# A new table of the order of all steps, and a new set of GpSimd's steps, in a fused attention, mixer and FNet kernel

## The chip, the cores and the metric

The kernel runs on one core of one Trainium2 chip. The metric is the device time of one execution in microseconds (us). A core has five engines that matter here, each with its own instruction queue, worked off strictly in order: TensorE (PE in the profile, with its weight loads as PEld), VectorE (DVE), ScalarE (ACT), GpSimd (POOL), and SyncE (SP), which here only issues DMAs. Engines wait for each other and for DMAs through semaphores. SBUF is the on-chip memory that holds operands, PSUM the one that TensorE writes its sums to.

## What is computed

Three stages, one after the other, in float32. The scale of q and k in the inputs is raised, which changes no shape.

```python
def _attn_ref(q, k, v, cap):                 # (4, 12, 448, 64)
    scores = np.matmul(q, k.transpose(0, 1, 3, 2)) / np.sqrt(64)
    scores = cap * np.tanh(scores / cap)     # cap 30
    attn = np.exp(scores - np.max(scores, axis=-1, keepdims=True))
    attn = attn / (np.sum(attn, axis=-1, keepdims=True) + 1e-09)
    return np.matmul(attn, v)

def _moe_ref(x, w_tok1, w_tok2, w_ch1, w_ch2):   # x (4, 448, 768)
    h = np.maximum(x.transpose(0, 2, 1) @ w_tok1, 0.0) @ w_tok2
    u = x + h.transpose(0, 2, 1)
    return u + np.maximum(u @ w_ch1, 0.0) @ w_ch2      # 768 -> 1536 -> 768

def _moe2_ref(x, w_ch1, w_ch2):
    u = x + np.real(np.fft.fft(np.fft.fft(x, axis=1), axis=2))
    un = (u - mean(u)) / np.sqrt(var(u) + 1e-06)       # over the 768
    return u + np.maximum(un @ w_ch1, 0.0) @ w_ch2     # 768 -> 3072 -> 768
```

## The kernel before

The kernel doesn't issue its instructions where the stages are written. The stages first record steps in a list; a step is one instruction or a few of one kind (one DMA, one vector operation, three or six matmuls), with the tiles that it reads and writes. There are 4196 steps, numbered in the order of recording. `Plan.run` then goes through the table `ORDER` and emits step after step; where a step may run on VectorE or on GpSimd, it goes to GpSimd if its number stands in the set `POOLED` and to VectorE otherwise. Since every engine works off its queue in order, `ORDER` alone sets what stands ahead of what on each engine, and an instruction that waits holds up all that stands behind it on its engine. Tile buffers are handed out in that order too.

```python
for k in ORDER:
    o = self.ops[k]
    ...
    o.fn("P" if k in POOLED else next(e for e in o.engines if e != "P" or len(o.engines) == 1))
```

The names that the rest needs:

- *Matrix products.* Each float32 operand is split into a high and a low part, and each product is three matmuls of 448 columns (`mm3`, lines 403 to 405): high weight by high data, high by low, low by high. `wh` and `wl` (or two tiles `raw`, `p`) are the weight parts, `u`, `r` and `y` data tiles, `mm` a PSUM tile of two halves of 448.
- *Weights.* A step on SP loads them (`raw<-in_m_dram`, line 464). Three ScalarE steps (line 431, `cv`, `raw`) and one VectorE step (line 472) rebuild their values; another pair of steps splits them into the two parts. Parts that are needed again are written to DRAM and fetched back (`kept`, lines 513 and 517).
- *Attention.* Scores `sc` (line 629), tanh on ScalarE (`t<-sc`, line 617), the maximum over partitions on GpSimd (`mb<-m`, line 669), the subtraction on VectorE, exp on ScalarE (line 677), then the product with v (`av`, line 727).
- *Output sums.* Twelve tiles `z` of 128 x 2 x 448 (z_76 to z_87 in the lists) hold the running result. What a second product of a layer leaves in PSUM is added to them by VectorE (`z<-mm,z`, here called a gather; a helper at line 434 records this and every other tensor_tensor, on VectorE and GpSimd alike). A PSUM tile is free for the next product when it has been gathered. At the end `z<-z` steps add pairs of tiles, and `store` (line 1335) writes each tile out, the last of them in two halves.
- *FNet.* `u<-mm,r` at line 1722 and `r<-y,r` at line 1735 are VectorE steps that form data tiles from transform sums; the normalisation stands between them and the last layer.

Of the kernel before, what the change touches and what calls it, by code (L numbers as in the profile page):

```python
# [58 lines left out]
class Op:  # L59
# [6 lines left out]
    2, 0, 3, 54, 4, 68, 69, 5, 1, 6, 55, 56, 7, 8, 10, 9, 57, 11, 12, 14, 13, 15, 20, 21, 58, 22, 16, 18, 23, 17, 19,  # L66
    73, 71, 30, 31, 59, 72, 74, 75, 77, 76, 78, 26, 81, 79, 32, 60, 29, 24, 27, 85, 25, 80, 28, 82, 33, 36, 34, 37,
    86, 39, 87, 95, 35, 38, 40, 121, 122, 70, 61, 88, 124, 41, 83, 42, 43, 84, 62, 44, 63, 45, 64, 46, 126, 96, 97,
    65, 47, 125, 66, 127, 48, 50, 130, 128, 91, 98, 89, 92, 49, 67, 94, 51, 138, 99, 93, 131, 129, 90, 52, 134, 132,
    106, 101, 139, 102, 140, 53, 104, 133, 135, 100, 103, 105, 141, 144, 197, 123, 196, 269, 172, 199, 136, 107, 108,  # L70
    137, 110, 109, 173, 174, 175, 207, 111, 142, 148, 145, 176, 149, 150, 151, 146, 177, 112, 200, 143, 115, 113, 178,
    114, 116, 147, 205, 117, 159, 154, 186, 188, 206, 208, 118, 120, 187, 189, 119, 152, 155, 203, 201, 204, 202, 153,
    190, 193, 272, 209, 270, 198, 179, 213, 214, 215, 157, 180, 191, 181, 156, 182, 210, 158, 216, 192, 223, 183, 217,
    160, 161, 211, 184, 194, 163, 212, 162, 218, 219, 164, 274, 165, 273, 275, 195, 224, 225, 185, 220, 322, 323, 271,
    787, 168, 166, 167, 169, 221, 226, 278, 170, 276, 234, 229, 171, 227, 279, 247, 249, 277, 248, 250, 230, 232, 286,
    222, 282, 280, 251, 254, 788, 789, 790, 281, 283, 228, 231, 284, 325, 235, 255, 285, 233, 256, 296, 287, 288, 297,
    298, 236, 327, 289, 292, 299, 302, 238, 252, 237, 239, 261, 253, 290, 791, 293, 240, 291, 792, 262, 326, 328, 241,
    267, 243, 333, 329, 265, 242, 295, 793, 244, 300, 339, 303, 334, 268, 294, 301, 330, 257, 245, 331, 340, 246, 305,
    304, 332, 306, 258, 341, 342, 794, 384, 324, 783, 510, 786, 383, 307, 308, 309, 337, 335, 795, 310, 338, 311, 336,
    345, 343, 346, 349, 350, 312, 386, 388, 344, 313, 387, 389, 266, 314, 316, 390, 392, 263, 259, 351, 315, 348, 317,  # L80
    352, 457, 385, 456, 347, 373, 375, 393, 391, 355, 318, 394, 396, 353, 374, 358, 319, 356, 320, 321, 376, 400, 401,
    402, 354, 260, 395, 397, 359, 357, 796, 360, 461, 398, 361, 399, 797, 362, 459, 403, 410, 411, 412, 404, 363, 405,
    364, 406, 413, 416, 365, 366, 460, 462, 264, 409, 407, 380, 367, 369, 465, 463, 368, 414, 370, 473, 466, 408, 464,
    415, 371, 377, 467, 471, 372, 474, 417, 419, 475, 509, 458, 378, 381, 468, 418, 434, 420, 472, 421, 422, 469, 423,
    518, 476, 425, 436, 470, 426, 512, 479, 379, 798, 382, 435, 477, 437, 482, 483, 484, 480, 485, 513, 519, 424, 427,
    448, 514, 516, 446, 430, 428, 643, 511, 570, 571, 486, 515, 517, 449, 478, 481, 447, 526, 527, 429, 528, 431, 487,
    489, 529, 438, 432, 520, 488, 521, 439, 490, 433, 492, 440, 524, 494, 522, 491, 523, 493, 525, 495, 496, 532, 535,
    530, 536, 537, 538, 533, 498, 497, 575, 573, 499, 503, 441, 539, 542, 500, 574, 576, 534, 531, 442, 501, 444, 577,
    579, 502, 540, 504, 545, 443, 587, 578, 445, 541, 580, 547, 581, 583, 505, 588, 543, 589, 506, 508, 507, 582, 544,
    546, 560, 562, 584, 450, 548, 549, 585, 590, 550, 451, 586, 551, 593, 645, 696, 572, 644, 646, 552, 648, 452, 558,  # L90
    591, 561, 594, 563, 596, 597, 598, 599, 595, 647, 649, 553, 592, 654, 650, 554, 660, 555, 600, 453, 655, 651, 603,
    564, 652, 454, 556, 653, 559, 601, 604, 661, 662, 557, 606, 656, 658, 602, 605, 565, 657, 659, 455, 607, 663, 670,
    566, 664, 671, 672, 609, 608, 610, 698, 697, 611, 665, 612, 699, 701, 613, 666, 673, 676, 700, 614, 702, 567, 617,
    615, 703, 707, 669, 667, 674, 616, 618, 679, 677, 668, 704, 708, 621, 623, 681, 705, 709, 619, 678, 710, 675, 706,
    680, 622, 624, 713, 620, 714, 715, 625, 682, 683, 711, 716, 626, 568, 684, 685, 712, 627, 569, 723, 724, 725, 717,
# [190 lines left out]
    3010, 3014, 3017, 3063, 3073, 3076, 3110, 3128, 3134, 3174, 3177, 3193, 3209, 3215, 3236, 3239, 3273, 3276, 3378,  # L286
    3385, 3409, 3434, 3446, 3456, 3501, 3517, 3519, 3521, 3524, 3539, 3552, 3564, 3574, 3577, 3589, 3655, 3661, 3664,
    3665, 3696, 3743, 3774, 3802, 3808, 3812, 3815, 3827, 3852, 3865, 3877, 3899, 3908, 3918, 3933, 3945, 3946, 3949,
    3951, 3952, 3981, 4018, 4065, 4115, 4121, 4142, 4166, 4181,
}  # L290


# [1857 lines left out]
```

## Time and profile before

| | us |
|---|---|
| median of 3 runs | 1377.07 |
| range of the runs | 1375.84 to 1378.19 |
| the profiled execution | 1376.16 |
| its span | 1374.4 |
| TensorE busy in the span | 1325.2 |
| VectorE, ScalarE, GpSimd busy | 1044.3, 763.7, 434.3 |
| mean granted TensorE clock, as a share of full | 0.989 |

The profiled execution took 1.8 us more than its span, which goes from the first to the last instruction that the profile shows. The last matmul ends at 1362.2 us in the span.

In rows of a timeline, the first two numbers are the start and the duration in us, then come engine, line, operation, output<-inputs and shape; in square brackets stand the idle time of the engine just before and what ended it. Matmuls overlap, so a busy TensorE is a queue of matmuls that begin one every 0.2 us.

### The profile page before, as it was taken

The numbers are of one execution on the slowest core, as the hardware profiler recorded it, in microseconds if no ns is written. First come the engines' busy times: TensorE is split into PE (matmuls) and PEld (weight loads), VectorE is DVE, ScalarE is ACT, GpSimd is POOL, SyncE is SP. The second block draws the span as 40 slices with busy tenths as digits, with TensorE's granted clock in tenths as the row PEclk, the third lists the DMA queues.
The fourth block names the chain that finished last, engine by engine and source line by source line (L and its number), as shares of the span: only waits on it lengthen the run. The fifth ranks groups of instructions, "written<-read, shape, count | busy, mean of one in ns | idle before, by whom it ended". The sixth has DMA issues, their size and how long they took to land.

```text
span 1374.4 us, 18462 instructions
## 1 busy us (share of the span) xinstructions
PE 1325.2 (96%) x7230; PEld 1098.7 (80%) x7230; DVE 1044.3 (76%) x1078; ACT 763.7 (56%) x926; POOL 434.3 (32%) x217
## 2 busy tenths in 40 slices
PE   7999999999999999999999999998989999999995
PEld 2345454599989899999889999998978889999984
DVE  6998988756656655878998895675899646865996
ACT  6888777687676566455444344543453453543431
POOL 3524344222120222101122544225551225324421
PEclk8999999999999999999999999999999999999998
DMA  4313211047798788887767623546463733333322
GB/s 147 95 64 142 68 41 55 1 164 252 278 315 295 261 313 308 294 300 255 252 235 249 246 98 117 177 164 205 139 227 134 260 117 93 126 103 112 107 69 81
DMA packets 74041, 239.18 MB, mean 174 GB/s; under 512 B 8322, under 2 KB 9730, under 8 KB 73826
## 3 DMA queue, kind: packets, MB, share of 16 engines
q1 hardware_dynamic: 73952, 238.00, 50.9%
q8 instruction: 57, 0.93, 0.3%
q14 instruction: 30, 0.25, 0.1%
q10 hardware_dynamic: 2, 0.00, 0.0%
HBM read 171.74 MB, written 69.56 MB: 176 GB/s over the span
## 4 chain that ended last, share of the span: by engine, by line
PE 67%; DVE 18%; ACT 7%; DMA 4%; issue 3%; SPq 0%; POOL 0%; DVEq 0%; ACTq 0%
PE mm L403 18%; PE mm L404 18%; PE mm L405 18%; DVE z L434 5%; PE av L727 3%; DVE m L434 3%; DMA raw<-in_m_dram 2%; PE sc L629 2%; DVE r L434 2%; ACT cv L431 2%; DVE u L434 2%; DVE t L434 1%; PE av L758 1%; PE mx L870 1%; ACT t L677 1%
## 5 line engine op out<-in xcount | busy, mean ns | idle before, releaser
L434 DVE TENSOR_TENSOR z<-mm,z 128x896 f32<-128x896 f32 (+1 forms) x205 | 198.4, 984 | 90.6 <-PE mm L405 85.0
L404 PE MATMUL mm<-u,wh 128*128 128x448 f32 x630 | 230.7, 366 | 0.5 <-DVE u L1722 0.5
L403 PE MATMUL mm<-u,wh 128*128 128x448 f32 x570 | 208.9, 366 | 0.9 <-issue 0.5
L405 PE MATMUL mm<-u,wl 128*128 128x448 f32 x570 | 208.3, 365 | 0.0
L403 PE MATMUL mm<-r,wh 128*128 128x448 f32 x504 | 185.6, 368 | 8.8 <-DVE z L434 8.8
L405 PE MATMUL mm<-r,wl 128*128 128x448 f32 x504 | 185.0, 367 | 0.0
L434 POOL TENSOR_TENSOR p<-p 128x768 f32<-128x768 f32 (+1 forms) x42 | 86.1, 2052 | 266.5 <-DMA kept<-p 98.7
L404 PE MATMUL mm<-r,wh 128*128 128x448 f32 x450 | 165.5, 368 | 1.3 <-DVE r L946 0.9
L669 POOL PARTITION_ALL_REDUCE mb<-m x48 | 105.3, 2244 | 156.2 <-DVE m L434 156.2
L404 PEld LDWEIGHTS mm<-u,wh 128*128 128x128 f32 x630 | 118.6, 188 | 10.3 <-DVE u L1722 0.7
L431 ACT ACTIVATE r<-mm 128x896 fp32r<-128x896 f32 (+5 forms) x86 | 70.4, 829 | 100.8 <-PE mm L405 68.9
L403 PEld LDWEIGHTS mm<-u,wh 128*128 128x128 f32 x570 | 107.3, 188 | 10.6 <-issue 0.8
L405 PEld LDWEIGHTS mm<-u,wl 128*128 128x128 f32 x570 | 107.2, 188 | 8.9
L403 PEld LDWEIGHTS mm<-r,wh 128*128 128x128 f32 x504 | 94.9, 188 | 19.5 <-DVE z L434 9.0
L431 ACT ACTIVATE cv<-raw 128x768 bf16<-128x768 int8 (+2 forms) x76 | 67.8, 892 | 73.9 <-DMA raw<-in_m_dram 48.9
L434 POOL TENSOR_TENSOR wl<-wl,wh 128x768 fp32r<-128x768 f32 x26 | 51.5, 1984 | 161.7 <-ACT wh L431 131.2
L405 PEld LDWEIGHTS mm<-r,wl 128*128 128x128 f32 x504 | 95.1, 189 | 8.1 <-POOL wl L434 0.3
L404 PEld LDWEIGHTS mm<-r,wh 128*128 128x128 f32 x450 | 84.8, 188 | 10.0 <-DVE r L946 2.4
L472 DVE SCALAR_TENSOR_TENSOR p<-raw 128x768 int32<-128x768 int32 x48 | 49.6, 1033 | 53.8 <-ACT raw L431 51.9
L434 DVE TENSOR_TENSOR t<-t,mb 128x1344 f32<-128x1344 f32 x48 | 79.1, 1662 | 4.5 <-POOL mb L669 4.4
L629 PE MATMUL sc<-qr 64*128 64x448 f32 x288 | 70.4, 594 | 9.7 <-ACT t L617 8.9
L431 ACT ACTIVATE raw<-raw 128x768 fp32r<-128x768 f32 x52 | 43.3, 839 | 64.4 <-DMA raw<-kept 64.4
(243 smaller groups left out, 3074.2 us busy)
## 6 DMA issues: line engine op xcount, KB each, us to landing
kept<-p SPq DMA_DIRECT2D x96, 384.0 KB, 4.8
raw<-in_m_dram SPq DMA_DIRECT2D x48, 767.6 KB, 5.5
wl<-kept SPq DMA_DIRECT2D x88, 384.0 KB, 3.8
raw<-kept SPq DMA_DIRECT2D x52, 384.0 KB, 3.1
raw<-in_c_dram SPq DMA_DIRECT2D x24, 767.6 KB, 5.9
p<-kept SPq DMA_DIRECT2D x30, 384.0 KB, 4.0
qr<-in_qk_dram SPq DMA_DIRECT2D x23, 448.0 KB, 4.1
wh<-kept SPq DMA_DIRECT2D x24, 384.0 KB, 4.4
```

The source lines that it names most:

```text
L403: T.matmul(out=dst, lhsT=wh, rhs=xh, start=first, stop=False, skip_group_check=more)
L404: T.matmul(out=dst, lhsT=wh, rhs=xl, start=False, stop=False, skip_group_check=more)
L405: T.matmul(out=dst, lhsT=wl, rhs=xh, start=False, stop=last, skip_group_check=more)
L431: pl.op(a(n), lambda e: A.activation(out=out(), in_=src(), func=func, **kw), reads, writes)
L434: pl.op(engs, lambda e: eng[e].tensor_tensor(out=out(), in0=in0(), in1=in1(), op=op), reads, writes)
L472: pl.op(v(cols), lambda e: V.scalar_tensor_tensor(out=value(I32), in0=raw()[:rows, :cols, 0], scalar=5, in1=field(), op0=ALU.logical_shift ...
L629: T.matmul(out=ps()[:, k, :S], lhsT=qr()[d, S + c * 128:S + (c + 1) * 128], rhs=qr()[d, :S], start=True, stop=True)
L669: pl.op({"P": 1.9}, lambda e, k=k: P.partition_all_reduce(mb()[:, k], mx()[:, k], 128, bass_isa.ReduceOp.max), [mx, mb], [kb], hold=0.75)
L677: pl.op(a(KC * S, 0.1), lambda e, k=k: A.activation(out=tl()[:, :, k], in_=tl()[:, :, k], func=AF.Exp, scale=cap_sb[:, 0:1]), [tl, "cap"], ...
L727: T.matmul(out=ps()[d, :S], lhsT=vv()[:, KC * p + c, d], rhs=tl()[:, c, hd], start=(c == 0), stop=False, skip_group_check=True)
L758: T.matmul(out=ps()[32 * k:32 * k + 32, :S], lhsT=ones[:, 0:32].bitcast(F32) if c < KC else half_ones[:, p], rhs=tl()[:, c, hd] if c < KC ...
L870: T.matmul(out=ps()[:, :S], lhsT=channels_of(rt()[:, tb, c], kc % NJ), rhs=wt[:, tb, :], start=False, stop=last, skip_group_check=True)
```

## The change

Two tables are replaced, `ORDER` and `POOLED`; no other line differs. TensorE and ScalarE carry out the same steps in another order, and SP issues the same DMAs in another order. GpSimd has 212 steps where it had 211, VectorE 1035 where it had 1036: some steps go to GpSimd that did not, and about as many come back.

```diff
 ORDER = [
-    2, 0, 3, 54, 4, 68, 69, 5, 1, 6, 55, 56, 7, 8, 10, 9, 57, 11, 12, 14, 13, 15, 20, 21, 58, 22, 16, 18, 23, 17, 19,
...
-    4165, 4160, 4115, 4166, 4150, 4184, 4161, 4149, 4155, 4190, 4167, 4168, 4186, 4171, 4187, 4191, 4192, 4151, 4157,
-    4169, 4139, 4170, 4163, 4172, 4156, 4188, 4162, 4193, 4194, 4185, 4173, 4174, 4175, 4189, 4195,
+    2, 0, 3, 54, 4, 68, 69, 1, 6, 8, 7, 9, 55, 10, 11, 56, 12, 14, 13, 15, 57, 20, 21, 22, 58, 16, 18, 23, 17, 19, 71,
...
+    4148, 4114, 4165, 4115, 4166, 4162, 4150, 4149, 4161, 4184, 4155, 4190, 4191, 4186, 4167, 4168, 4171, 4187, 4192,
+    4193, 4151, 4157, 4169, 4139, 4170, 4163, 4172, 4156, 4188, 4194, 4185, 4195, 4173, 4174, 4175, 4189,
...
 POOLED = {
...
-    729, 806, 808, 814, 824, 866, 893, 930, 955, 967, 984, 1029, 1115, 1134, 1145, 1152, 1191, 1204, 1334, 1354, 1377,
+    729, 806, 808, 822, 845, 866, 893, 930, 955, 984, 999, 1017, 1074, 1115, 1134, 1145, 1152, 1191, 1202, 1204, 1334,
```

The order shows in three places.

**ScalarE at the start.** Its first steps, before and then after. `t<-sc` and `te<-sc` are tanh of scores, `cv<-raw`, `cv<-cv`, `raw<-cv` and `w1h<-raw` belong to the first mixer weights, which a DMA brings, and `t<-t,cap_sb` is exp.

```order
L431 ACTIVATE cv_307<-raw_291 112x512 [waits DMAHW3_49]
L431 ACTIVATE cv_307<-cv_307 112x512 [waits Activation_49]
L617 ACTIVATE t_310<-sc_304,scl_75 128x896 [waits DVE_49,PE_49]
L617 ACTIVATE t_310<-sc_312,scl_75 128x896 [waits PE_49]
L431 ACTIVATE raw_291<-cv_307 112x512 [waits Activation_49]
```

```order
L617 ACTIVATE t_308<-sc_302,scl_75 128x896 [waits DVE_49,PE_49]
L617 ACTIVATE t_308<-sc_305,scl_75 128x896 [waits PE_49]
L431 ACTIVATE cv_311<-raw_291 112x512 [waits DMAHW3_49]
L617 ACTIVATE t_308<-sc_313,scl_75 128x896 [waits PE_49]
L431 ACTIVATE cv_311<-cv_311 112x512 [waits Activation_49]
```

The two steps on the mixer weights, which stood ahead of the first tanh, now stand behind the second and the third. Some fifteen steps further on, one tanh (`t_387<-sc_376` before, `t_382<-sc_370` after) stood behind the first exp and now stands ahead of it.

**VectorE in the FNet stage**, before and then after. `r_8054<-r_8054,r_8004` before and `u_8056<-u_8056,r_7982` after are the same step, a difference of two tiles fetched from DRAM; z_79 is gathered right behind it in both.

```order
L434 TENSOR_TENSOR z_81<-mm_8032,z_81 128x448 [waits PE_49]
L434 TENSOR_TENSOR r_8054<-r_8054,r_8004 128x896 [waits DMAHW7_49,DMAHW2_49]
L434 TENSOR_TENSOR z_79<-mm_8042,z_79 128x448 [waits PE_49]
L434 TENSOR_TENSOR wl_8050<-wl_8050,wh_8049 128x768 [waits DMAHW5_49,Activation_49,Pool_49]
L434 TENSOR_TENSOR z_80<-mm_8042,z_80 128x448 [waits PE_49]
```

```order
L434 TENSOR_TENSOR r_8068<-mm_7997,u_7840 128x896
L434 TENSOR_TENSOR wl_8054<-wl_8054,wh_8053 128x768 [waits DMAHW0_49,Activation_49]
L434 TENSOR_TENSOR u_8056<-u_8056,r_7982 128x896 [waits DMAHW3_49,DMAHW1_49]
L434 TENSOR_TENSOR z_79<-mm_8085,z_79 128x448 [waits PE_49]
L434 TENSOR_TENSOR r_7982<-u_8056 128x448 [waits DVE_49,Pool_49]
L434 TENSOR_TENSOR raw_7980<-raw_7980 128x768 [waits DMAHW2_49,Activation_49]
L434 TENSOR_TENSOR raw_8051<-raw_8051 128x768 [waits DMAHW7_49,Activation_49]
L434 TENSOR_TENSOR u_8158<-mm_8073,y_8061 128x896 [waits PE_49]
```

Before, the product that fills the other half of mm_8042 (three matmuls by three, TensorE's next step) needs the gather of z_79 done. After, TensorE's product behind this gather waits for an earlier one, and 15 steps of three matmuls of the first layer stand behind it until the first that needs `u_8158`, the last row shown.

**VectorE at the end**, its last rows before (but the very last) and then after. mm_11183 before and mm_11187 after are the PSUM tile whose two halves end in z_84, the tile that is stored in two halves.

```order
L434 TENSOR_TENSOR z_80<-mm_11117,z_80 128x448 [waits PE_49]
L434 TENSOR_TENSOR z_84<-mm_11183,z_84 128x448 [waits PE_49]
L434 TENSOR_TENSOR z_85<-z_85,z_79 128x896 [waits DVE_49]
L434 TENSOR_TENSOR z_86<-z_86,z_80 128x896 [waits DVE_49]
L434 TENSOR_TENSOR z_85<-mm_11190,z_85 128x448 [waits DVE_49]
L434 TENSOR_TENSOR z_87<-z_87,z_78 128x896
L434 TENSOR_TENSOR z_86<-mm_11190,z_86 128x448 [waits DVE_49]
L434 TENSOR_TENSOR z_87<-z_87,z_81 128x896 [waits DVE_49]
L434 TENSOR_TENSOR z_87<-mm_11210,z_87 128x448 [waits DVE_49]
L434 TENSOR_TENSOR z_83<-z_83,z_80 128x448
L434 TENSOR_TENSOR z_83<-mm_11203,z_83 128x896 [waits DVE_49]
L434 TENSOR_TENSOR z_84<-z_84,z_81 128x448
```

```order
L434 TENSOR_TENSOR z_84<-mm_11187,z_84 128x448 [waits PE_49]
L434 TENSOR_TENSOR z_84<-mm_11187,z_84 128x448
L434 TENSOR_TENSOR z_85<-z_85,z_79 128x896 [waits DVE_49]
L434 TENSOR_TENSOR z_86<-z_86,z_80 128x896 [waits DVE_49]
L434 TENSOR_TENSOR z_85<-mm_11207,z_85 128x448 [waits DVE_49,PE_49]
L434 TENSOR_TENSOR z_87<-z_87,z_78 128x896
L434 TENSOR_TENSOR z_86<-mm_11207,z_86 128x448 [waits DVE_49]
L434 TENSOR_TENSOR z_87<-z_87,z_81 128x896 [waits DVE_49]
L434 TENSOR_TENSOR z_87<-mm_11220,z_87 128x448 [waits DVE_49,PE_49]
L434 TENSOR_TENSOR z_83<-z_83,z_80 128x448
L434 TENSOR_TENSOR z_83<-mm_11200,z_83 128x896 [waits DVE_49,PE_49]
```

Before, one more row stands behind those shown, the second gather of z_84, and TensorE fills mm_11183 with its last six matmuls. After, `z_84<-z_84,z_81` stands some rows ahead of those shown, both gathers of z_84 are next to each other, and the six matmuls that complete mm_11187 stand ahead of the last five steps of six matmuls; the last of all fills mm_11200.

## Rows read from the trace of the kernel before

**Rows 1.** The page: busy time of each engine and its share of the span

```profile
PE 1325.2 (96%) x7230; PEld 1098.7 (80%) x7230; DVE 1044.3 (76%) x1078; ACT 763.7 (56%) x926; POOL 434.3 (32%) x217
```

**Rows 2.** Stretches of the span: busy us (x instructions) of each engine, granted clock (PEclk)

```profile
0.00:50.00 50.00, 39.47 (x218) 14.82 (x222) 36.31 (x38) 34.73 (x40) 20.60 (x14) 0.90 0.43 137
900.00:1060.00 160.00, 150.35 (x716) 136.13 (x715) 133.28 (x122) 70.54 (x91) 70.15 (x35) 0.98 0.51 171
1362.20:1374.40 12.20, 0.00 (x0) 0.00 (x0) 9.10 (x12) 0.00 (x0) 0.00 (x0) 0.58 0.58 226
480.20:483.60 3.40, 3.40 (x11) 3.01 (x10) 0.82 (x1) 0.19 (x1) 0.00 (x0) 0.50 0.95 335
944.50:947.90 3.40, 3.38 (x9) 3.04 (x10) 2.15 (x2) 0.00 (x0) 3.32 (x3) 0.51 0.03 5
```

**Rows 3.** What TensorE waited for: us in total, times, longest

```profile
PE mm L403 <- DVE z L434: 15.7, 12, 3.6
PE sc L629 <- ACT t L617: 8.9, 5, 3.3
```

**Rows 4.** Timeline of TensorE: matmuls behind seven of its longer idle times

```profile
10.03 1.86 PE L629 MATMUL sc<-qr 64*128 64x448 f32 x4 [3.21 <-ACT t L617]
...
28.16 1.02 PE L629 MATMUL sc<-qr 64*128 64x448 f32 x4 [3.29 <-ACT t L617]
...
478.93 0.47 PE L403 MATMUL mm<-r,wh 128*128 128x448 f32 x1 [2.18 <-DVE z L434]
...
944.52 0.74 PE L403 MATMUL mm<-r,raw 128*128 128x448 f32 x1 [3.57 <-DVE z L434]
...
1017.87 0.45 PE L403 MATMUL mm<-r,wh 128*128 128x448 f32 x1 [2.08 <-DVE z L434]
...
1029.18 0.47 PE L403 MATMUL mm<-y,wh 128*128 128x448 f32 x1 [1.47 <-DVE z L434]
...
1037.08 0.47 PE L404 MATMUL mm<-u,p 128*128 128x448 f32 x1 [1.35 <-DVE u L434]
```

**Rows 5.** Timeline of ScalarE in the first 30 us

```profile
7.76 0.66 ACT L431 ACTIVATE cv<-raw 112x512 bf16<-112x512 int8 x1 [5.03 <-DMA raw<-in_tok_dram]
...
8.99 1.89 ACT L617 ACTIVATE t<-sc,scl 128x896 f32<-128x896 f32 x2
...
25.80 1.42 ACT L677 ACTIVATE t<-t,cap_sb 128x1344 f32<-128x1344 f32 x1 [2.01 <-DVE t L434]
```

**Rows 6.** The chain that ended last, in order of time, around 470 and 940 us

```profile
466.83 7.23 DMA raw<-in_m_dram
...
476.91 0.96 DVE p L472
...
932.01 0.20 PE mm L404
...
935.17 6.58 DMA r<-kept
```

**Rows 7.** Timeline of VectorE at four places

```profile
941.85 2.08 DVE L434 TENSOR_TENSOR r<-r 128x896 f32<-128x896 f32 x1 [2.06 <-DMA r<-kept]
...
1004.68 1.07 DVE L434 TENSOR_TENSOR u<-mm,u 128x896 f32<-128x896 f32 x1
...
1014.46 2.72 DVE L434 TENSOR_TENSOR r<-u,r 128x896 fp32r<-128x896 f32 x1
...
1017.64 1.07 DVE L1722 SCALAR_TENSOR_TENSOR u<-mm,r 128x896 fp32r<-128x896 f32 x1
...
1345.36 1.08 DVE L434 TENSOR_TENSOR z<-z 128x896 f32<-128x896 f32 x1
...
1362.20 0.62 DVE L434 TENSOR_TENSOR z<-mm,z 128x448 f32<-128x448 f32 x1 [7.06 <-PE mm L405]
```

**Rows 8.** Timeline of GpSimd around 941 us

```profile
940.91 2.07 POOL L434 TENSOR_TENSOR y<-y,r 128x896 f32<-128x896 f32 x1 [1.82 <-DMA r<-kept]
```

**Rows 9.** DMA issues of the last 14 us: count, KB each, median us to landing

```profile
out_dram<-z SPq DMA_DIRECT2D x5, 448.0 KB, 2.5
```

432 rows, old and new, of tables (ORDER, POOLED) are left out of this document.

## The prediction

> **What bounds the kernel now.** The page comes first: TensorE is busy for 1325.2 us [rows 1] of a span of 1374.4. The change takes no matmul away, so what can be won is the 49.2 us in which TensorE stands. Of these, 12.2 lie behind the last matmul [rows 2], about 1 ahead of the first, and 36 in between. The list of its waits says for whom: 15.7 us for gathers of z by VectorE in 12 waits, 8.9 for tanh on ScalarE in 5, the rest in small pieces [rows 3]. Third come the stretches: 10.5 of the 49.2 us fall into the first 50 us and 9.65 into 900 to 1060 us, where VectorE is busy for 133.28 of 160 [rows 2]; in the long stretches between, TensorE waits rarely. Fourth, the granted clock: behind a long wait it drops to half, 1.2 instead of 2.4 GHz, as in 480.2 to 483.6 (0.50) and 944.5 to 947.9 (0.51) [rows 2]. TensorE had stood 2.18 and 3.57 us before [rows 4]. 3.40 us at half the clock do the work of 1.7, so such a wait costs its length and about 1.7 us more.
>
> So the question is, wait by wait, whether the new order removes what ends it, and what it makes late instead.
>
> **The start.** The first ScalarE step on the mixer weights waits for their DMA until 7.76, and tanh, which stands behind it, begins at 8.99 [rows 5]; TensorE stands 3.21 us for it [rows 4]. After the change tanh stands ahead of that step and waits for its scores alone. At 25.80 exp had waited 2.01 us for VectorE with the next tanh behind it [rows 5], and TensorE stood 3.29 us [rows 4]; this tanh now stands ahead of exp. That removes up to 6.5 us, and some of the half clock. But in this stretch VectorE is busy for 36.31 and ScalarE for 34.73 of 50 us [rows 2], and both must bring the same maxima and exps before the first products with v; what TensorE gains early it partly waits for there. Ends 0 and 6.5; I take 3, the middle, since the two engines are busy 70%.
>
> **Around 477 us.** VectorE's step on a weight needs a DMA that took 7.23 us and three ScalarE steps behind it; it runs from 476.91 to 477.87 [rows 6], and the gather that TensorE wants only after it. TensorE stands 2.18 us [rows 4]. In the new order the weight step still stands ahead of this gather, with one more VectorE step between. But TensorE meets the product that needs it later: I count 12 steps of six matmuls and 19 of three from the same point, where there were 10 and 10, so 129 matmuls instead of 90. At 0.20 us for each (the chain's step from one matmul to the next at full clock [rows 6]) this is 7.8 us of further work ahead of it, against 2.18 us of wait and one VectorE step of about 1. The wait goes, and its 1.7 us of half clock: 3.9. Ends 0, if the DMA is issued that much later too, and 3.9; I take 3.9, since 7.8 stands against 3.2.
>
> **Around 941 us.** This is the case of the second lists of the change: a difference of two fetched tiles waits 6.58 us for a DMA [rows 6]; it then takes 2.08 us [rows 7], while GpSimd works from 940.91 to 942.98 [rows 8], and the gather of z_79 stands behind. TensorE stands 3.57 us [rows 4]. Afterwards the same difference still stands ahead of the same gather, but TensorE needs nothing behind it for 15 steps of three matmuls, 45 by 0.2, or 9 us. The wait and its half clock go: 5.3. Ends 3.6, if half of the DMA's wait comes back, and 5.3; I take 5.3.
>
> **1004 to 1037 us.** Here VectorE itself is late. Three waits of 2.08, 1.47 and 1.35 us [rows 4], 0.9 us in pieces, and one drop of the clock, 1.7: some 7.5. Its steps are long: 2.72 us at 1014.46 for a sum of two tiles of 896, where the same form alone takes 1.08 [rows 7]. At 941.85 a step that takes 1.08 alone needed 2.08, and it ended 0.95 us behind GpSimd's end [rows 7, 8]: a VectorE step with two inputs in SBUF stands while a GpSimd step runs. Before, eleven steps from 1004.68 to the one that ends at 1018.71 took 14.0 us [rows 7]. The new order gives one of GpSimd's steps here to VectorE and moves gathers forward: counted at unstretched lengths, VectorE has ten steps and 10.1 us to do ahead of that same step's end, plus what two GpSimd steps of about 2 [rows 8] hold it up, 0 to 4, against 60 matmuls or 12.0 us. The middle is 12.1, level with TensorE. Ends 0 and 7.5; I take 2.8: 1.9 for VectorE's path, 14.0 to 12.1, and half of the clock's 1.7.
>
> The Trainium skill, page "SBUF — State Buffer", section "SBUF: two separate sides", has the pair of ports that VectorE and GpSimd share as an exclusive lock: who starts first holds it for a whole instruction, and the other waits. The trace agrees: 2.08 against 1.08 us, behind a GpSimd step of 2.07 [rows 7, 8]. By that rule an order can choose who waits but not remove the wait, which is the first rival below: by it the sum comes to 1368, by the places one by one to 1363.
>
> **Smaller waits.** Of the 15.7 us for z [rows 3] the four named take 9.3 [rows 4]; eight waits hold 6.4. Their gathers or the products behind them have moved by some steps in half of the places. Ends 0 and 6.4; I take 3.
>
> **The end.** VectorE's gather at 1362.20 had waited 7.06 us for the last matmul [rows 7]; it is of the tile that TensorE fills last, and eleven VectorE steps stand behind it. They are 9.10 us of work [rows 2] and end 9.2 us behind the last matmul. Then a store follows; full ones land in 2.5 us [rows 9]. Now both gathers of this tile wait for a product that stands five steps of six matmuls, 30 by 0.2 or 6.1 us, ahead of the end. The same VectorE work, less one step of 0.6 that has moved further forward, starts 6.1 earlier and ends about 2.5 us behind the last matmul instead of 9.2. The last store is a full one instead of a half, some 0.55 us longer. That is 6.7 less 0.55, about 6. Ends 4, if the last gathers wait for the matmuls of the end one by one, and 7.
>
> **New waits.** Where the new order brings VectorE later than before, I find two places by counting steps: one in the middle (the deviation ahead of the last layer), about 1.5, and one where 1040 us was, about 1.8. Together +3.3, counted as above: VectorE's steps at their unstretched lengths against the matmuls at 0.2 us. The order shows no durations of DMAs, and other new waits will hang on them. Of the 36 us in between, the seven waits of [rows 4] are 17.2, and 18.8 lie all over in smaller ones; I charge 7 for new ones, between 0 and 18.8.
>
> **The sum.** 1376.16 for the profiled execution; less 3, 3.9, 5.3, 2.8, 3 and 6, which is 24.0; plus 3.3 and 7: 1362.5. The median of the runs stands 0.9 above the profiled execution, so 1363.
>
> **Rivals.**
> - *The lock only moves.* GpSimd has 212 steps instead of 211, so VectorE stands as often; the gains between 300 and 1310 us (15.0 by my sum) are spent by new waits of the same kind, and with the 3.3 and the 7 charged to nothing further, only start and end remain, 9: 1368. For it: VectorE is busy 76% of the whole span [rows 1]. Against: in the places at 477 and 941 a DMA was the cause, and there it's TensorE's own order that has changed. 0.17.
> - *The end does not shorten.* Another late VectorE step holds the last gathers: my sum without the 6, or 1369. Against it: VectorE had stood idle for 7.06 us just there [rows 7]. 0.07.
> - *Slower.* A step that waits for a DMA of 7 us stands ahead of a gather in new places, as at 477 and 941. Each costs up to 3.6 and the 1.7 of half clock, 5.3. Three more such places than I charge, 16, outweigh the net gain of 14: from there on it is slower; with four, 21, it is 1384. For it: SP's queue is reordered too, so DMAs may be issued later against their users. Against: TensorE had only two such places in 1374 us. 0.07.
> - *It nets to nothing*: between these, two to three such places, 1376. 0.07.
>
> **How the numbers follow.** The forecast has 0.62, centred on 1363, with its own range of 1354 to 1371. With the start's best end (6.5 for 3) and no new waits beyond the 3.3 it is 1353; with 18.8 of new waits instead of 7 it is 1375. These are the ends of the range: left out are the last two cases, 0.14, and some 0.05 beyond the lower end. About 0.2% (2.8 us) is what a measurement of this kernel can tell. Forecast, lock and end are all faster by more: 0.62, 0.17 and 0.07 make 0.86; same 0.07; slower 0.07.
>
> **What would show it.** Right: no TensorE wait over 2 us between 300 and 1310 us, in particular none on z around 470 to 490 and 930 to 950; a stretch behind the last matmul of about 6 us instead of 12.2; a mean of the granted clock above 0.989; TensorE's waits on tanh under 5 us in all. The lock: VectorE's two-input steps stay stretched and TensorE's waits for z stay near 15.7 us in other places. Wrong: a z gather behind a DMA-fed VectorE step with a wait of over 3 us, or a last gather that still waits 7 us for the last matmul with ten steps behind it.

## The result

| | before | after |
|---|---|---|
| median, us | 1376.45 (4 runs) | 1352.57 (4 runs) |
| range, us | 1373.63 to 1378.19 | 1350.48 to 1352.92 |
| ratio | | 0.9825 (95%: 0.9805 to 0.9845) |
| profiled execution and span, us | 1376.16, 1374.4 | 1350.48, 1348.7 |
| TensorE busy in the span, us | 1325.2 | 1319.9 |
| mean granted clock | 0.989 | 0.996 |

The change makes the kernel 24 us faster. The forecast was 14 us, 1363, with a range that began at 1353. On two other chips the changed kernel was at 0.985 and 0.983 of before. So the direction was right and the size was short by 10 us. The measured 1352.57 lies 0.4 us below the range, less than its own interval is wide (1349.6 to 1355.1), and the ratios of the other chips would be 1354 and 1355 us here, inside it.

The page of after, busy time by engine, answers to [rows 1]:

```profile
PE 1319.9 (98%) x7230; PEld 1096.9 (81%) x7230; DVE 1023.0 (76%) x1077; ACT 762.9 (57%) x926; POOL 442.8 (33%) x218
```

The same 7230 matmuls are busy for 5.3 us less: that is half clock which is gone. TensorE stands for 28.8 us of the span, where it stood for 49.2. VectorE is busy for 21.3 us less with practically the same instructions, GpSimd for 8.5 more.

The stretches, as in [rows 2]; the third is the one behind the last matmul, the last two lie behind waits of TensorE:

```profile
0.00:50.00 50.00, 41.86 (x251) 15.12 (x255) 41.81 (x42) 37.88 (x42) 25.33 (x16) 1.00 0.41 136
900.00:1060.00 160.00, 155.58 (x757) 141.41 (x756) 132.53 (x133) 74.68 (x94) 69.35 (x33) 1.00 0.58 193
1342.10:1348.70 6.60, 0.00 (x0) 0.00 (x0) 2.98 (x4) 0.00 (x0) 0.00 (x0) 0.80 0.56 220
482.00:485.40 3.40, 3.34 (x10) 3.01 (x11) 2.00 (x3) 0.80 (x1) 0.00 (x0) 0.56 0.93 349
1012.80:1016.20 3.40, 3.35 (x16) 3.12 (x17) 3.40 (x4) 0.00 (x0) 0.00 (x0) 1.00 0.03 5
```

Idle time of TensorE in the first 50 us fell from 10.5 to 8.1 us and its clock rose from 0.90 to 1.00; from 900 to 1060 it fell from 9.65 to 4.4; behind the last matmul 12.2 became 6.6. What TensorE waited for, as in [rows 3]:

```profile
PE mm L403 <- DVE z L434: 7.9, 4, 2.4
PE sc L629 <- ACT t L617: 3.2, 7, 1.1
```

And its longest waits that are left, in the timeline of TensorE, as in [rows 4]:

```profile
39.93 1.92 PE L629 MATMUL sc<-qr 64*128 64x448 f32 x8 [1.13 <-ACT t L617]
...
482.06 0.47 PE L403 MATMUL mm<-r,wh 128*128 128x448 f32 x1 [2.06 <-DVE z L434]
...
691.28 0.88 PE L1300 MATMUL mm<-r,ones 112*128 112x448 f32 x3 [1.43 <-DVE r L434]
...
1012.85 0.47 PE L403 MATMUL mm<-u,raw 128*128 128x448 f32 x1 [2.28 <-DVE z L434]
...
1331.77 0.44 PE L403 MATMUL mm<-y,raw 128*128 128x448 f32 x1 [2.35 <-DVE z L434]
```

The span fell by 25.7 us, and it can be split: 14.8 are waits between the first and the last matmul (36 became 21), 5.6 the end, 5.3 the clock. It is 1.8 us more than between the medians, since the profiled execution of after is the fastest of its four.

### The profile page after: what moved, and what is told of

The parts are those of the page before. It is cut to its first block, busy times and chain, and to the rows that moved or that the text cites. A ratio compares the mean times of both kernels' runs of the same rounds, so it can differ in the third digit from the quotient of the medians.

```text
span 1348.7 us, 18479 instructions
## 1 busy us (share of the span) xinstructions
PE 1319.9 (98%) x7230; PEld 1096.9 (81%) x7230; DVE 1023.0 (76%) x1077; ACT 762.9 (57%) x926; POOL 442.8 (33%) x218
## 4 chain that ended last, share of the span: by engine, by line
PE 82%; DVE 13%; ACT 2%; issue 1%; DMA 1%; POOL 0%; ACTq 0%; DVEq 0%; SPq 0%; POOLq 0%
PE mm L403 24%; PE mm L404 23%; PE mm L405 23%; DVE t L434 3%; DVE m L434 3%; PE av L727 2%; PE sc L629 2%; DVE z L434 2%; PE mx L870 2%; PE av L758 1%; DMA raw<-in_m_dram 1%; DVE u L434 1%; DVE te L434 1%; PE av L770 1%; DVE xl L434 1%
## 5 line engine op out<-in xcount | busy, mean ns | idle before, releaser
L403 PE MATMUL mm<-u,wh 128*128 128x448 f32 x612 | 224.5, 367 | 0.0
L405 PE MATMUL mm<-u,wl 128*128 128x448 f32 x612 | 224.1, 366 | 0.4 <-DVE wl L434 0.4
L404 PE MATMUL mm<-u,wh 128*128 128x448 f32 x606 | 221.8, 366 | 0.3 <-DVE u L434 0.3
L434 POOL TENSOR_TENSOR p<-p 128x768 f32<-128x768 f32 (+1 forms) x47 | 99.1, 2111 | 274.9 <-DMA kept<-p 96.1
L403 PE MATMUL mm<-r,wh 128*128 128x448 f32 x480 | 176.6, 368 | 2.1 <-DVE z L434 2.1
L405 PE MATMUL mm<-r,wl 128*128 128x448 f32 x480 | 176.3, 367 | 0.0
L404 PE MATMUL mm<-r,wh 128*128 128x448 f32 x456 | 168.3, 369 | 0.0
L431 ACT ACTIVATE r<-mm 128x896 fp32r<-128x896 f32 (+4 forms) x80 | 65.3, 823 | 114.9 <-PE mm L405 81.8
L405 PEld LDWEIGHTS mm<-u,wl 128*128 128x128 f32 x612 | 115.2, 188 | 10.5 <-DVE wl L434 0.8
L403 PEld LDWEIGHTS mm<-u,wh 128*128 128x128 f32 x612 | 115.2, 188 | 10.1 <-issue 0.3
L404 PEld LDWEIGHTS mm<-u,wh 128*128 128x128 f32 x606 | 113.8, 188 | 10.3 <-DVE u L434 0.7
L403 PEld LDWEIGHTS mm<-r,wh 128*128 128x128 f32 x480 | 90.6, 189 | 11.2 <-DVE z L434 3.3
L434 POOL TENSOR_TENSOR wl<-wl,wh 128x768 fp32r<-128x768 f32 x29 | 57.9, 2003 | 104.5 <-ACT wh L431 104.5
L431 ACT ACTIVATE wh<-wl 128x768 fp32r<-128x768 f32 x66 | 55.0, 839 | 57.7 <-DMA wl<-kept 57.7
L617 ACT ACTIVATE t<-sc,scl 128x896 f32<-128x896 f32 x72 | 70.3, 1004 | 14.0 <-PE sc L629 11.7
```

The lines of the kernel that those rows point to most:

```text
L403: T.matmul(out=dst, lhsT=wh, rhs=xh, start=first, stop=False, skip_group_check=more)
L404: T.matmul(out=dst, lhsT=wh, rhs=xl, start=False, stop=False, skip_group_check=more)
L405: T.matmul(out=dst, lhsT=wl, rhs=xh, start=False, stop=last, skip_group_check=more)
L431: pl.op(a(n), lambda e: A.activation(out=out(), in_=src(), func=func, **kw), reads, writes)
L434: pl.op(engs, lambda e: eng[e].tensor_tensor(out=out(), in0=in0(), in1=in1(), op=op), reads, writes)
L617: pl.op(a(W2, 0.06), lambda e: A.activation(out=out(), in_=ps()[:, :, :S], func=AF.Tanh, scale=scl[:, 0:1]), [ps, "cap", *reads], writes)
```

## The experiments

Each starts from one of the two kernels and changes only `ORDER` and `POOLED`. Both tables hold the same steps in their first 66, 1076, 2100, 3133, 3587 and 4157 entries, so a piece of the new order can stand in the old one. Where a piece of `ORDER` is changed, GpSimd's set among its steps goes with it. Differences in us are ratios to the kernel before on the same chip, times its 1375 us.

**The start alone.**

```diff
-ORDER = BEFORE
+ORDER = AFTER[:66] + BEFORE[66:]
```

> The kernel before, with only the first 66 entries of the order (and GpSimd's steps among them) taken from the changed kernel; both tables hold the same 66 steps there. Theory 'places' (each stretch of the table brings its own gain, waits and half clock together): at the same point of the program the changed kernel is 5.9 us ahead at the end of this piece and 6.6 later, so this alone gives 6 us, about 1370.5, with a granted clock of 1.00 over the first 50 us. Rival 'paid back' (the prediction's term): VectorE and ScalarE are busy to 70 per cent there and TensorE waits later for what it gained, so 3 us remain, about 1373.5, with new waits of over 2 us between 25 and 60 us.

Measured: 1372.7, ratio 0.9978 (0.9962 to 0.9993), 3.0 us less. The clock of the first 50 us is 1.00 in its profile, as expected, but on the median the gain is that of the prediction, and its waits that in after stand at 40 and 49 us are 1.61 each, not the over 2 us of the rival. The bookkeeping by two profiles gave too much because TensorE's first wait differs from one execution of the old order to the next. It was 3.21 us in the profile of before [rows 4]; the same wait, in the runs of the end alone and of the remaining pieces:

```profile
8.38 1.02 PE L629 MATMUL sc<-qr 64*128 64x448 f32 x4 [1.18 <-ACT t L617]
```

```profile
10.09 1.02 PE L629 MATMUL sc<-qr 64*128 64x448 f32 x4 [3.91 <-ACT t L617]
```

So a difference between two profiles, like the 5.9 and 6.6 us, holds the length of that one wait in one execution.

**The end alone.**

```diff
-ORDER = BEFORE
+ORDER = BEFORE[:4157] + AFTER[4157:]
```

> The kernel before, with only the last 39 entries of the order taken from the changed kernel. Theory 'places': the stretch behind the last matmul falls from 12.2 to about 6.6 us and nothing else changes, 5.6 us less, about 1370.9. Rival: in the old order the gathers ahead of these steps come later, VectorE is not free for the early gather, and no more than 2 us are won, 1374.5 or more.

Measured: 1370.96, ratio 0.9968 (0.9955 to 0.9982), 4.4 us less. The stretch behind the last matmul, 1365.03 to the end of its span:

```profile
1365.03:1371.60 6.57, 0.00 (x0) 0.00 (x0) 2.99 (x4) 0.00 (x0) 0.00 (x0) 0.76 0.56 222
```

It is 6.57 us instead of 12.2, with 2.99 us of VectorE's work instead of 9.10 [rows 2]. The mechanism stands by itself.

**New order, old set; old order, new set.**

```diff
-ORDER, POOLED = AFTER, AFTER
+ORDER, POOLED = AFTER, BEFORE
```

> The changed order with GpSimd's old set of steps. Theory 'order' (the gain is in what stands ahead of what): within 2 us of the changed kernel, 1352 to 1355, VectorE's busy time within 6 us of 1023. Theory 'lock' (VectorE's steps are stretched by GpSimd's, and the new set avoids it): VectorE's busy time goes back to about 1044 us and 6 to 9 us are lost, 1359 to 1362.

```diff
-ORDER, POOLED = BEFORE, BEFORE
+ORDER, POOLED = BEFORE, AFTER
```

> The old order with GpSimd's new set of steps: the other half of the run with the new order and the old set. Theory 'a pair' (order and set only fit together; that run lost 20 of the 24 us, though VectorE's busy time stayed at 1024): TensorE's waits between its first and last matmul rise from 36 to 45 us or more, and the kernel gets slower than before, by 5 to 15 us, 1380 to 1390. Rival 'lock': the new set alone takes stretching away, and it is 2 us or more faster than before.

Measured: 1374.1, ratio 0.9987 (0.9974 to 1.0001), and 1395.85, ratio 1.0146 (1.0119 to 1.0174). Set alone costs 20 us, order alone gives 2, both together 24. Both theories of the first run fell, and the second cost more than the 5 to 15 us expected. The first page is of the new order with the old set, the second of the old order with the new set:

```profile
PE 1325.9 (97%) x7230; PEld 1098.9 (80%) x7230; DVE 1024.1 (75%) x1078; ACT 762.7 (56%) x926; POOL 440.6 (32%) x217
```

```profile
PE 1331.2 (95%) x7230; PEld 1099.3 (79%) x7230; DVE 1053.1 (76%) x1077; ACT 763.0 (55%) x926; POOL 441.4 (32%) x218
```

VectorE's 1024.1 us are those of after, although the set is the old one. So it is the order that takes the stretching of VectorE's steps away, and yet TensorE stands 43.9 us of a span of 1369.8 (28.8 in after). In the other run it stands 63.4 of 1394.6 (49.2 in before). A table that doesn't fit the other costs some 15 us of waits either way. In the new order with the old set 9.0 us are waits for steps that can run on either of the two engines, differences of weight tiles and data tiles; after has 0.7 of the first row's kind and none of the other two:

```profile
PE mm L405 <- DVE wl L434: 4.0, 4, 2.9
...
PE mm L405 <- POOL wl L434: 2.6, 1, 2.6
PE mm L404 <- POOL u L434: 2.4, 2, 2.1
```

**One number of the set.** What one misfit costs:

```diff
 POOLED = AFTER
-    3397
```

> The changed kernel with a single number taken out of GpSimd's set, so that one difference of two weight tiles at 1054 us runs on VectorE, where it stands in the queue ahead of sums and gathers and waits for ScalarE. Theory 'a pair': VectorE stands from about 1051 to 1054 for it, the gather that TensorE wants comes 4 us later, and the wait of 3.3 us that the run with the whole old set showed at this place comes back, with the half clock: 2 to 4 us slower than the changed kernel. Rival: VectorE has time to spare there, and nothing changes beyond 1 us.

> The changed kernel, as the reference of the run before on the same chip: 1351 to 1355, 0.982 to 0.985 of the kernel before.

Measured: 1357.0 beside 1351.46 for the changed kernel on that chip, ratios 0.9874 (0.9852 to 0.9896) and 0.9834 (0.9814 to 0.9855): 5.5 us for one of 212 steps. The six executions lie between 1352.15 and 1361.16, those of the changed kernel between 1350.03 and 1352.96, so that the 2 to 4 us expected are not excluded. The profile is that of the slowest execution; VectorE with one step moved:

```profile
1053.27 0.96 DVE L434 TENSOR_TENSOR raw<-raw 128x768 fp32r<-128x768 f32 x1 [3.72 <-ACT raw L431]
1054.14 0.62 DVE L434 TENSOR_TENSOR z<-z 128x448 f32<-128x448 f32 x1
1054.68 0.95 DVE L434 TENSOR_TENSOR wl<-wl,wh 128x768 fp32r<-128x768 f32 x1
1055.55 2.69 DVE L434 TENSOR_TENSOR z<-z 128x896 f32<-128x896 f32 x1
1058.28 0.62 DVE L434 TENSOR_TENSOR z<-mm,z 128x448 f32<-128x448 f32 x1
```

GpSimd and TensorE there:

```profile
1054.91 2.38 POOL L434 TENSOR_TENSOR wl<-wl,wh 128x768 fp32r<-128x768 f32 x1 [20.47 <-ACT wh L431]
```

```profile
1059.05 0.44 PE L403 MATMUL mm<-u,raw 128*128 128x448 f32 x1 [3.29 <-DVE z L434]
```

The moved step waits 3.72 us for ScalarE at the head of VectorE's queue. What stood behind it shifts back, so that a sum of two tiles now meets a GpSimd step that it had missed, and takes 2.69 us instead of 1.08 [rows 7]; the gather of 1058.28 comes that much later, and TensorE stands 3.29 us. In the changed kernel beside it the same step waits on GpSimd, and TensorE has no wait of 1 us or more from 1039 to 1332 us.

**One exchange of neighbours in the old order.**

```diff
-    ... 2966, 2963, 2933, 2960, 3029 ...
+    ... 2966, 2963, 2960, 2933, 3029 ...
```

> The kernel before with one pair of neighbours exchanged: on VectorE the gather of z_79 at 943.85 stands ahead of the difference that waits for a DMA, instead of behind it. Theory 'what stands ahead': the gather runs when its matmuls end, at about 941.0, the wait of 3.57 us falls under 1 and the half clock behind it goes, 4.6 us less, about 1371.8. Rival: the difference is itself waited for soon after, so that the wait moves by a few matmuls and under 2 us are won, 1374.5 or more.

Measured: 1372.53, ratio 0.9975 (0.9960 to 0.9989), 3.4 us less. VectorE there; the second row is the gather, the third the difference:

```profile
941.05 0.63 DVE L434 TENSOR_TENSOR z<-mm,z 128x448 f32<-128x448 f32 x1 [2.03 <-PE mm L405]
942.87 0.62 DVE L434 TENSOR_TENSOR z<-mm,z 128x448 f32<-128x448 f32 x1 [1.20 <-PE mm L405]
943.41 1.16 DVE L434 TENSOR_TENSOR r<-r 128x896 f32<-128x896 f32 x1
```

The gather now waits for its matmuls alone and TensorE doesn't stand at all. The 3.57 us of [rows 4] was again one execution: with the old order at this place the other profiles show between 1.75 and 2.90.

**Four pieces alone.** For entries A to B:

```diff
-ORDER = BEFORE
+ORDER = BEFORE[:A] + AFTER[A:B] + BEFORE[B:]
```

Entries 3133 to 3586:

> The kernel before, with entries 3133 to 3586 of the order (about 996 to 1148 us) and GpSimd's set among these steps taken from the changed kernel. Theory 'stretch by stretch' (order and set together, each stretch for itself): at the same point of the program the changed kernel gains 4.6 us in this piece, so 4 to 5 us less than before, with VectorE's stretched steps down by some 10 us in 900 to 1060. Rival 'coupled' (the gain hangs on what the stretches around bring): under 2 us.

Measured: 1369.85, ratio 0.9966 (0.9947 to 0.9985), 4.7 us less, with VectorE busy for 1032.2 us. Entries 1076 to 2099:

> The kernel before, with entries 1076 to 2099 (about 379 to 681 us) and the set among these steps from the changed kernel. By the two profiles this piece gains 1.9 us. Theory 'stretch by stretch': 2 us less, and the wait at 477 comes back at the product behind it, about 2.1 us and the half clock, as in the changed kernel. Rival (the prediction's term): the waits at 396 and 477 go with their half clock and nothing comes instead, 5 us less.

Measured: 1373.41, ratio 0.9992 (0.9974 to 1.0010); the wait did come back at a later product, 1.85 us at 484. Entries 2100 to 3132:

> The kernel before, with entries 2100 to 3132 (about 681 to 996 us) and the set among these steps from the changed kernel. By the two profiles this piece gains 5.4 us, nearly all at the wait of 3.57 us at 941 with its half clock. Theory 'stretch by stretch': 4 to 5.4 us less. Rival: the single exchange of the gather and the difference, run alone, left the rest as it was and gave 3.4 on the median; if the wait varies from run to run, this gives no more than that, 3 to 3.5.

Measured: 1375.97, ratio 1.0011 (0.9996 to 1.0026), no gain, against both. The wait at 941 is gone, but just past the end of the piece TensorE meets this one:

```profile
997.25 0.74 PE L403 MATMUL mm<-u,p 128*128 128x448 f32 x1 [4.94 <-ACT u L431]
```

Entries 66 to 1075 and 3587 to 4156:

> The kernel before, with entries 66 to 1075 and 3587 to 4156 of the order (about 25 to 379 and 1148 to 1350 us) and the set among these steps from the changed kernel: the two pieces that no run has had yet. Theory 'stretch by stretch': by the two profiles they give 0.7 and 3.8, so 4.5 us less. Theory 'pair with its neighbours': the five other pieces gave 3.0, 1.1, -1.5, 4.6 and 4.4 alone, 11.6 of 24; if pieces only pay beside each other, these two give under 3, and the rest of the 24 belongs to no piece.

Measured: 1372.66, ratio 0.9980 (0.9961 to 0.9998), 2.8 us less; this doesn't tell the two apart. The six pieces alone make 14.5 us of 21 to 24.

**Joined pieces.** Entries 2100 to 3586 in one, and 1076 to 3586 in one:

> The kernel before, with entries 2100 to 3586 of the order (about 681 to 1148 us) and the set among these steps from the changed kernel: the two pieces of which one alone gave 4.6 and the other lost 1.5, in one. Theory 'seams' (a piece pays where it meets the other order: TensorE stood 4.94 us at 992, two steps past the end of the losing piece, for a ScalarE step behind a DMA): without the seam between them they give 8 to 10 us, by the two profiles 10.0, so 1365 to 1367. Rival 'the pieces' own': 3 us, the sum of the two alone, about 1372.

> The same with entries 1076 to 3586 (about 379 to 1148 us), three pieces in one. Theory 'seams': 11 to 13 us, by the two profiles 11.9, about 1363; with 3.0 for the start, 2.7 for the rest and 4.4 for the end that is the 21 to 24 us of the whole change. Rival: 4.2, the sum of the three alone, about 1371, and some 8 us of the change stay without a place.

Measured: 1366.7, ratio 0.9941 (0.9921 to 0.9961), 8.1 us less where the two alone make 3.2; and 1366.53, ratio 0.9944 (0.9923 to 0.9964), 7.7 us less. The first speaks for the seam: TensorE has no wait of 1 us or more between 732 and 1019 us in its profile, the one of 4.94 us is gone, and without it the piece pays. The second lies between its theories: the piece from 379 to 681 us adds nothing that can be measured. Start, rest, these and the end make 17.9 us; the rest of the 21 to 24 is no more than the intervals of four runs together leave open.

**Further in the same direction.** Four steps moved forward in the changed kernel, then three more:

```diff
-    1460, 1461, 1462, 1463, 1447, 1384, 1400, 1465, 1464, 1385, 1341, 1304,
+    1460, 1461, 1462, 1341, 1463, 1447, 1384, 1400, 1465, 1464, 1385, 1304,
...
-    3263, 3121, 3221, 3224, 3218,
+    3263, 3224, 3121, 3221, 3218,
...
-    4160, 4154, 4148, 4114, 4165, 4115, 4166, 4162, 4150, 4149, 4161,
+    4160, 4148, 4154, 4114, 4165, 4115, 4166, 4149, 4162, 4150, 4161,
```

> The changed kernel with four VectorE or ScalarE steps moved forward at the three longest waits that are left: at 480 the gather that TensorE waits for ahead of the weight step that waits for a DMA; at 1010 the gather of another tile ahead of a sum of 2.25 us; at 1329 the last-layer copy and gather that free the PSUM tile ahead of two others. Theory 'what stands ahead': 2.06, 2.28 and 2.35 us go, with the half clock behind the first and the last, 6 to 9 us less than the changed kernel. Rival: each wait moves to the next step behind, 2 us or less.

```diff
-    3203, 3245, 3174, 3177, 3307, 3304, 3305, 3306, 3283, 3284, 3285, 3286, 3292, 3282,
+    3203, 3174, 3177, 3307, 3304, 3305, 3306, 3283, 3284, 3285, 3286, 3292, 3245, 3282,
...
-    4160, 4148, 4154, 4114, 4165, 4115, 4166, 4149,
+    4165, 4160, 4148, 4154, 4114, 4166, 4115, 4149,
```

> The changed kernel with the four moves of the run before and three more: at 1037 two gathers ahead of a sum of two tiles, and at the end one weight copy on ScalarE and its difference on GpSimd ahead of others. Theory 'what stands ahead': the waits of 1.16 and 1.06 us go too, 2 us less than with the four moves and 5 less than the changed kernel, 1346 to 1348. Rival: each such wait moves on, no difference from the changed kernel, 1351 to 1353.

> The changed kernel itself once more, beside the kernel before on this chip. Theory: its ratio to before is that of the first comparison, 0.981 to 0.984, 1350 to 1353, and its executions lie closer together than those of before, since the waits on DMAs that differ from one execution of before to the next (the first one at 7 us, those at 396 and 477) are gone. Rival: the four executions of the first comparison were a lucky sample, and it is 1356 or more.

Measured: four moves 1348.91, ratio 0.9809 (0.9782 to 0.9835); seven moves 1346.09, ratio 0.9797 (0.9767 to 0.9826); the changed kernel beside the latter 1354.56, ratio 0.9847 (0.9819 to 0.9875), above the 1350 to 1353 us expected. The four moves ran on a chip without the changed kernel; by the ratios they gain 2 to 5 us on it, less than the 6 to 9 expected and within the intervals. The seven moves are 8.5 us faster than the changed kernel and beat both kernels; their executions (1345.4 to 1350.1) don't meet those of the changed kernel (1351.7 to 1355.5). What TensorE waits for with seven moves:

```profile
PE mm L403 <- ACT wh L431: 2.8, 2, 2.6
...
PE mm L403 <- DVE z L434: 1.4, 2, 1.2
```

The waits for z, 7.9 us in after, are down to 1.4; one new wait stands in the first row, 2.63 us at 491.68 for weights that ScalarE copies.

## Why the prediction was short

**The step that failed is "New waits", the flat 7 us for waits without a place.** The sum took away 24.0 us and put 10.3 back: 3.3 for two places and the flat 7. That the change gave 24, just what the sum took away, is luck, since single terms were off both ways. For all places that it names (start, 477, 941, 1004 to 1037, the end and the two new waits) the sum makes 17.7 us less; the start alone, entries 1076 to 3586 in one and the end alone make 15.1. For what has no named place it makes 4 us more: 7 for new waits, less 3 for smaller ones that go. There the kernel gained: 2.8 us in the run of the two remaining pieces, and 6 to 9 by what is left of 21 to 24. Without the 7 the sum would have given 1356.

The waits show the same. The two counted places are there: 1.43 us at 691.28, forecast 1.5; and 1.16 at 1037, forecast 1.8. The 7 is not: behind the first 50 us TensorE has no new wait of 1.1 us or more at a place that the prediction doesn't name. One of the eight smaller waits for z grew, from 1.48 us at 1353.15 to 2.35 at 1331.77, both 42 matmuls ahead of the end; the other seven are not there. Waits of 1.1 us and more between first and last matmul are 13 with 24.7 us in before and seven with 11.7 in after; all shorter ones make 11.2 and 9.4. So the 18.8 us that the prediction called smaller, with six of the 13 among them, shrank where 4 more were forecast. Waits and end without the clock were to fall by 9.4 us by my sum (13.7 and 6, less 10.3) and fell by 20.4.

The reason that I gave, that new waits hang on durations which an order doesn't show, holds where tables don't fit: a seam cost 4.94 us, a set that doesn't belong to its order some 15 us of waits, a single number of it 5.5. But I charged it to a pair of tables that were changed together, and as a flat sum from the idle time of before, without a place. What would have been the better reading: a charge for new waits needs a place and a releaser, and where none is found it belongs into the range and not into the sum.

Of the signs that I had named for being right, three are there: 6.6 us behind the last matmul, a mean clock of 0.996, 3.2 us of waits on tanh. The first is not: TensorE waits over 2 us at 482.06 and 1012.85.

Step by step:

- **Start**, forecast 3, alone 3.0: right, and for the reason given, since two waits, 6.5 us together, went, TensorE's idle time in the first 50 us fell by 2.4 only, and the half clock went beside it. ScalarE begins tanh at 5.54 instead of 8.99 [rows 5] and the weight step stands behind it:

```profile
5.54 1.90 ACT L617 ACTIVATE t<-sc,scl 128x896 f32<-128x896 f32 x2 [2.78 <-PE sc L629]
7.33 0.67 ACT L431 ACTIVATE cv<-raw 112x512 bf16<-112x512 int8 x1
```

- **477 us**, forecast 3.9: wrong. TensorE does pass the product of [rows 4] without a wait, but stands 2.06 us at the next one that needs a free PSUM tile. VectorE in after:

```profile
478.31 0.96 DVE L472 SCALAR_TENSOR_TENSOR p<-raw 128x768 int32<-128x768 int32 x1 [4.52 <-DMA kept<-p]
479.19 0.95 DVE L434 TENSOR_TENSOR p<-p 128x768 f32<-128x768 f32 x1
480.06 0.95 DVE L434 TENSOR_TENSOR wl<-raw,wh 128x768 fp32r<-128x768 f32 x1
480.92 2.08 DVE L434 TENSOR_TENSOR z<-mm,z 128x896 f32<-128x896 f32 x2
```

It is the next weight step, which again stands idle, 4.52 us, with the gather behind it. The row puts this down to a DMA that stores the tile; ScalarE's last step on the weight's data ended at 478.28, just ahead of it, too. I followed the one gather and not the ones behind it. The clock behind it is 0.56: nothing was won here, and the piece from 379 to 681 us alone gave 1.1 or nothing. There was little to win, either: the 2.18 us were one execution's. In six other runs with the old order and set there the wait is between nothing and 1.40 us; in the run of the exchange:

```profile
478.41 0.47 PE L403 MATMUL mm<-r,wh 128*128 128x448 f32 x1 [0.45 <-DVE z L434]
```

- **941 us**, forecast 5.3: the mechanism is right (the exchange of two neighbours does it), the size is 3.4 on the median, since the profile had caught a long one.
- **1004 to 1037 us**, forecast 2.8 and 1.8 back: the piece gives 4.7 alone. VectorE's path was shortened more than I took, because its steps are stretched less. In the run of this piece alone VectorE is busy for 125.96 us where it was for 133.28 [rows 2], with one instruction more:

```profile
900.00:1060.00 160.00, 152.42 (x725) 137.65 (x724) 125.96 (x123) 71.51 (x90) 67.15 (x34) 0.98 0.51 173
```

The groups of VectorE's steps in the whole kernel, first before, then after:

```profile
L434 DVE TENSOR_TENSOR z<-z 128x896 f32<-128x896 f32 (+1 forms) x60 | 64.6, 1104 | 0.4
L434 DVE TENSOR_TENSOR wl<-wl,wh 128x768 fp32r<-128x768 f32 x38 | 49.8, 1317 | 8.7 <-ACT wh L431 8.6
```

```profile
L434 DVE TENSOR_TENSOR z<-z 128x896 f32<-128x896 f32 (+1 forms) x60 | 54.5, 933 | 2.8 <-ACT z L431 2.2
L434 DVE TENSOR_TENSOR wl<-wl,wh 128x768 fp32r<-128x768 f32 x37 | 44.4, 1200 | 6.2 <-ACT wh L431 6.0
```

The same 60 sums of output tiles take 10.1 us less, at 933 instead of 1104 ns each. The half clock of this place, of which I took half, cost nothing: in the run of the end alone, with the old order here, the clock stays at 1.00 behind the wait of 2.07 us, and the next wait is longer by what was won, 3.00 us instead of 1.47 [rows 4]. VectorE, whose gather begins at 1027.90 there and at 1028.05 in before, sets the time:

```profile
1017.70:1021.10 3.40, 2.89 (x13) 2.48 (x14) 3.37 (x4) 0.35 (x1) 0.00 (x0) 1.00 0.65 218
```

```profile
1029.03 0.47 PE L403 MATMUL mm<-y,wh 128*128 128x448 f32 x1 [3.00 <-DVE z L434]
```

- **The end**, forecast 6: 5.6 by the stretches, 4.4 (2.5 to 6.2) alone. Some of it was paid back at a place that I hadn't looked at: the wait of 1.48 us at 1353.15 is 2.35 in the run of the end alone, as in after, and the clock behind it is 0.51. First before, then the run of the end alone:

```profile
1353.15 0.47 PE L403 MATMUL mm<-r,raw 128*128 128x448 f32 x1 [1.48 <-DVE z L434]
```

```profile
1354.70 0.65 PE L403 MATMUL mm<-r,raw 128*128 128x448 f32 x1 [2.35 <-DVE z L434]
```

Two of VectorE's last steps in after; only the last gather of all needs the last matmul, which ended at 1342.1, and it began 2.1 us behind it:

```profile
1339.68 0.62 DVE L434 TENSOR_TENSOR z<-mm,z 128x448 f32<-128x448 f32 x1 [0.49 <-PE mm L405]
...
1344.20 1.09 DVE L434 TENSOR_TENSOR z<-mm,z 128x896 f32<-128x896 f32 x1
```

- **The clock**: 1.7 us for a drop fits the rows that are left (0.56 over 3.4 us behind 482.0 is 1.5) where TensorE sets the time, and is nothing where VectorE does, as at 1019; three drops of the middle went (at 480, 941 and 1019) and two came (at 482 and 1331), and the half clock of the start went too.

**The rivals.** "The lock only moves" fell: VectorE's busy time went down by 21.3 us with one GpSimd step more, and TensorE's waits for z fell from 15.7 to 7.9. The Trainium skill, page "SBUF — State Buffer", section "SBUF: two separate sides", has the ports that the two share as an exclusive lock: the instruction that starts first holds them to its end, and the other blocks. The sum of 2.69 us behind GpSimd's 2.38 agrees with it (it ended 0.95 us behind GpSimd's end). That an order can't remove such waits was my addition, and it is wrong: with the new order and the old set VectorE's busy time fell by 20.2 us, with the same steps on each engine. "Slower", by weight steps that wait for a DMA ahead of a gather, happened at one place (482), not at three. Its mechanism is the right one for the misfits: it is what the moved step of 3397 did.

What stays open: how far the pieces add up. Joined ones make 17.9 us of 21 to 24, and intervals of 2 to 3 us each don't tell whether the remainder is a gain of the whole or noise. That TensorE waits least with the new pair, and more in both crossed runs, was measured; why this pair fits at every place was not explained.

## What to carry to other kernels

An order and an assignment to engines are one object: cost them together. Here the order alone kept 2 of 24 us, and the set alone lost 20. Follow every gather behind a step that waits for a DMA or another engine, not only the first that was late, and ask what stands at the head of the queue when its data is not there. Put a price on a wait only where you can name its place and its releaser, and before a single wait of a profile is priced, ask whether a DMA stands behind it: one such wait was between 1.2 and 3.9 us in executions of the same order, another between nothing and 2.2. And ask which engine sets the time behind a drop of the clock: where it was VectorE, the drop cost nothing.

## What the runs showed of the hardware

Waits behind steps that a DMA feeds differ from one execution to the next. At 395 us such a weight step stands ahead of the gather. The profile of before had a wait of 1.2 us there; the runs of the end alone and of the remaining pieces, with the same order there, show these:

```profile
396.58 0.74 PE L403 MATMUL mm<-r,wh 128*128 128x448 f32 x1 [2.54 <-DVE z L434]
```

```profile
396.94 0.74 PE L403 MATMUL mm<-r,wh 128*128 128x448 f32 x1 [3.24 <-DVE z L434]
```

And a wait of the same length doesn't always cost the clock: behind 2.06 us in after it fell to 0.56 (482.0 to 485.4), behind 2.28 us at 1012.85 it stayed at 1.00, in the rows on the stretches above. Not even the same wait of the same kernel always does: in another execution of the changed kernel, on another chip, the latter is 2.30 us, and the clock behind it is 0.53:

```profile
1016.30:1019.70 3.40, 3.36 (x9) 3.01 (x10) 3.40 (x4) 0.00 (x0) 0.00 (x0) 0.53 0.02 5
```
